# Attention scores in 64-row tiles of the array, two heads per step, with shifted key and score steps

## The chip, the cores and the metric

The kernel runs on one core of a Trainium2 chip. A core has five engines, each with its own queue of instructions, worked off in order: TensorE (PE in the profile, with PEld for the loading of its stationary operand), VectorE (DVE), ScalarE (ACT), GpSimd (POOL) and SyncE (SP, used here only to issue transfers). PE writes to PSUM, and ACT or DVE carry the results from there to SBUF. The metric is the device time of one execution in microseconds.

## The reference

A pooled attention is followed by a maxout feed-forward layer. Eight batches, eight heads, 576 queries of dimension 64. Keys and values are averaged over groups of 8 positions, so that there are 72 of each.

```python
k_p = k.reshape(B, H, Sp, pool, D).mean(axis=3)          # 72 pooled keys
v_p = v.reshape(B, H, Sp, pool, D).mean(axis=3)
scores = scale * np.matmul(q, k_p.transpose(0, 1, 3, 2))  # 576 x 72 per head
attn = np.exp(scores - max); attn = attn / attn.sum(...)
x = np.matmul(attn, v_p)            # heads side by side: 4608 tokens x 512
h = np.maximum(np.maximum(x @ w1, x @ w2), x @ w3)        # 4608 x 768
out = h @ w_out                                           # 4608 x 512
```

## The kernel before, in words

The 4608 tokens are worked in nine blocks of 512 (`block`, line 436). A block has two parts: `hidden` (line 315) forms the three products with w1, w2, w3 for six groups of 128 hidden columns, and `project` (line 327) multiplies by w_out for four groups of 128 tokens. Each part is a generator that yields after each group of matmuls. One such stretch is called a slot here: in `hidden` a slot is four matmuls into a PSUM tile `pw` (line 299), and the slots go round w1, w2, w3; in `project` it is six matmuls into `po` (line 335). Blocks 2 to 8 have 18 + 4 = 22 slots, block 1 has 25 and block 0 has 34, since their first tokens are worked in smaller parts. The tile of w1 is copied to SBUF by ACT (`t`, line 305), VectorE takes the maximum with the second (line 308) and the third (line 311, into `hT`). The tag `pw` has three PSUM buffers.

The attention of a later batch is done between the slots. A plan, a dictionary from slot number to steps, is written out by hand: for block 0 in the call of `block` at line 451, for the others in `plan` (line 460), where block n works on batch n + 1. After a slot's matmuls have been issued, its steps are issued by `do` (line 258), so the place of a step in the plan is its place in the queue of every engine that it uses. The steps that matter here are these.

- `a` (line 281): VectorE adds the two halves of the raw keys of batch 1 into `k16`. `K` (`pool_k`, line 189): four matmuls finish the pooling of these keys in PSUM (`pkp`), and VectorE and then ACT copy them into the two copies in `kps` (lines 196 and 197).
- `k` (`turn_k`, line 183): for batches 1 and 2, six transposes on PE (`pkt`, line 174); for later ones the transposed keys `kT` have been made by a DMA transpose (`Z`, line 272, on SP's queue). Two copies then fill `kz` (line 179), on ACT, for batch 2 on VectorE. `kz` holds for each head the 64 rows of its keys either in partitions 0 to 63 or in 64 to 127 (the parity); the other half is zero. There are two `kz`, for even and odd batches.
- `q` and `Q`: transposes of queries on PE for batch 1, copied out by ACT or VectorE. `T` (line 268): the queries of a later batch by DMA transpose on SP's queue. The transposed queries hold two 64-row groups in the 128 partitions, and a group of 64 queries lies in the lower or upper half by its parity.
- `s` (`scores`, line 213): one head. Three matmuls with all 128 rows (line 203), of 320, 192 and 64 columns; the zero half of `kz` cancels the queries of the other parity. The first has one parity and the other two the other. They fill 576 columns of a PSUM tile `psc` (two banks; tag `att`, two buffers), and ACT takes the exponential of all 576 in one instruction (line 208) into `et`.
- `v` (`values`, line 235): eight matmuls of 65 columns into a tile of tag `att`, reciprocal and multiplication on VectorE into `xn`. `x` and `X` (`turn_x`, line 220): the transpose of `xn` into `xT`, which the next blocks read; on PE for batches 0 and 1, by DMA transpose on SP's queue for the others.

GpSimd loads and pools keys and values of a batch to come (`pool_work`, line 472); its loads wait for the first matmuls of a block. The results go out by DMAs from SP's queue (line 345), the last ones partly from ACT's. For batch 0, before block 0, the scores are formed by functions of their own (lines 381 and 387), which use `score` (line 199).

Of the kernel before, what the change touches and what calls it, by code (L numbers as in the profile page):

```python
# [14 lines left out]
def kernel(  # L15
# [11 lines left out]
    nc = tc.nc  # L27
    dt = mybir.dt
    F32, BF16, F16 = dt.float32, dt.bfloat16, dt.float16

    B, H, S, D = q.shape
    POOL = 8
    Sp = S // POOL
    C = H * D
# [7 lines left out]
    NG = 9  # L42
# [4 lines left out]
    TOK = B * S  # L47
# [7 lines left out]
    psp = ctx.enter_context(tc.tile_pool(name="psp", bufs=1, space=PSUM))  # L55
    ctx.enter_context(tc.manual_schedule())

    kts, vts, qbs, kps, qTs, kTs, ets = {}, {}, {}, {}, {}, {}, {}
# [52 lines left out]
    for i in range(3):  # L111
        if i == 2:
# [5 lines left out]
        out=wo_sb, in_=moe_w_out.rearrange("(jc p) c -> p jc c", p=128))  # L118
# [5 lines left out]
    kz_all = [const.tile([128, 2, H, 128], BF16, name=f"kz{i}", tag=f"kz{i}")  # L124
              for i in range(2)]
# [15 lines left out]
    def new_kp(b):  # L141
        kps[b] = sb2.tile([96, 6, 2, D], BF16, name="kp", tag="kp")
# [17 lines left out]
    def turn_q(b, n0, n1, evac, tag):  # L160
        if b not in qTs:
            qTs[b] = sb2.tile([128, 2 * NG, 128], BF16, name="qT", tag="qT")
        pqt = psp.tile([128, n1 - n0, 128], BF16, name="pqt", tag=tag[0],
                       bufs=tag[1])
        qf = qbs[b].rearrange("p hp t d -> p (hp t d)")
        for n in range(n0, n1):
            nc.tensor.transpose(pqt[:, n - n0, :], qf[:, 128 * n:128 * n + 128],  # L167
                                ident)
        evac(out=qTs[b][:, n0:n1, :], in_=pqt)
# [13 lines left out]
    def turn_k(b):  # L183
        pkt = keys(b, TR) if b < 3 else kTs[b]
        for par in range(2):
            fill_kz(b, par, 0, H, pkt,
                    nc.vector.tensor_copy if b == 2 else nc.scalar.copy)

    def pool_k(b, tag):

        new_kp(b)
        pkp = psp.tile([128, 6, D], F32, name="pkp", tag=tag[0], bufs=tag[1])
        for j in range(4):
            nc.tensor.matmul(pkp, identh[0:96, :], k16[:, :, j, :],  # L194
                             start=(j == 0), stop=(j == 3))
        nc.vector.tensor_copy(out=kps[b][:, :, 0, :], in_=pkp[0:96])
        nc.scalar.copy(out=kps[b][:, :, 1, :], in_=pkp[0:96])

    def score(b, h, out, tp, i0, i1):

        f = NG * (h // 2) + tp
        n = f // 2
        nc.tensor.matmul(out, kz_all[b % 2][:, f % 2, h, :],  # L203
                         qTs[b][:, n + i0:n + i1, 64 * (h % 2):64 * (h % 2) + 64],
                         start=True, stop=True)

    def exp(out, in_):
        nc.scalar.activation(out=out, in_=in_, func=FT.Exp, scale=1.0 / 64.0)  # L208

    def new_et(b):  # L210
        ets[b] = sb2.tile([Sp, H, S], F16, name="et", tag="et")

    def scores(b, h):
        psc = psp.tile([128, 1024], F32, name="psc", tag="att", bufs=2)
        score(b, h, psc[:, 0:320], 0, 0, 5)
        score(b, h, psc[:, 320:512], 1, 0, 3)
        score(b, h, psc[:, 512:576], 1, 3, 4)
        exp(ets[b][:, h, :], psc[0:Sp, 0:S])

    def turn_x(b, c0, keep, xn, tag, evac=nc.scalar.copy):  # L220
        if b > 1:
# [13 lines left out]
    def values(b, c0):  # L235
        pav = psp.tile([128, 2, 512], F32, name="pav", tag="att", bufs=2)
        for h in range(H):
            nc.tensor.matmul(  # L238
                pav[:, h // 4, 65 * (h % 4):65 * (h % 4) + 65],
                ets[b][:, h, c0:c0 + 128], vp_all[:, b, h, :],  # L240
                start=True, stop=True)
        pv = pav[:, :, 0:260].rearrange("p g (h e) -> p g h e", e=65)
        rcp = sb3.tile([128, 2, 4], F32, name="rcp", tag="rcp")
        nc.vector.reciprocal(out=rcp, in_=pv[:, :, :, 64])  # L244
        xn = sb3.tile([128, 2, 4, D], F16, name="xn", tag="xn", bufs=6)
        nc.vector.tensor_tensor(  # L246
            out=xn, in0=pv[:, :, :, 0:D],
            in1=rcp.to_broadcast([128, 2, 4, D]), op=ALU.mult)
        return xn
# [8 lines left out]
    def do(b, steps):  # L258

        for name in steps.split():
            i = int(name[1:] or 0)
            if name[0] in "qQ":
                turn_q(b, *QS[i], nc.vector.tensor_copy if name[0] == "Q"
                       else nc.scalar.copy, TR)
            elif name[0] == "T":
                qTs[b] = sb2.tile([128, 2 * NG, 128], BF16, name="qT", tag="qT")
                nc.sync.dma_start_transpose(  # L270
                    out=qTs[b], in_=qbs[b].rearrange("p hp t d -> p (hp t d)"))
            elif name[0] == "Z":
                kTs[b] = sb2.tile([128, 6, 96], BF16, name="kT", tag="kT")
                nc.sync.dma_start_transpose(
                    out=kTs[b], in_=kps[b].rearrange("p i a d -> p (i a d)"))
            elif name[0] == "k":
                turn_k(b)
            elif name[0] == "K":
                pool_k(b, PW)
            elif name[0] == "a":  # L280
                nc.vector.tensor_tensor(out=k16, in0=kts[b][:, :, 0:4],  # L281
                                        in1=kts[b][:, :, 4:8], op=ALU.add)
            elif name[0] == "s":
                if i == 0:
                    new_et(b)
                scores(b, i)
            elif name[0] == "v":
                xns[b, i] = values(b, CHUNKS[i][0])
            else:
                turn_x(b, *CHUNKS[i], xns[b, i], TR,  # L290
                       nc.vector.tensor_copy if name[0] == "X" else nc.scalar.copy)
# [35 lines left out]
    def project(n, hT):  # L327
        for mm in range(4):
            m = 4 * n + mm
            last = m == TOK // 128 - 1  # L330
            osb = sb3.tile([128, C], F32, name="osb", tag="osb", bufs=5)
            for c in ((slice(0, C // 2), slice(C // 2, C)) if last else (slice(0, C),)):
                po = psp.tile([128, c.stop - c.start], F32, name="po", tag="pw", bufs=3)
                for jc in range(JCH):
                    nc.tensor.matmul(po, hT[:, jc, bass.ts(mm, 128)], wo_sb[:, jc, c],  # L335
                                     start=(jc == 0), stop=(jc == JCH - 1))
                if last:
                    nc.vector.tensor_copy(out=osb[:, c], in_=po)
                else:
                    nc.scalar.copy(out=osb[:, c], in_=po)  # L340
                for u in range(2):
                    b, g = divmod(2 * m + u, NG)
                    dst = out[S * b:S * b + S, :].rearrange("(r g) c -> r g c", g=NG)
                    e = nc.scalar if last and (u or c.start == 0) else nc.sync
                    e.dma_start(out=dst[:, GS[g], c], in_=osb[64 * u:64 * u + 64, c])
            yield

# [15 lines left out]
    for i in range(0, 6, 2):  # L363
        src = kts[0][:, i:i + 2] if i else kt0
        f = const.tile([96, 2, 4, D], F32, name="kf", tag="kf")
# [5 lines left out]
            out=kps[0][:, i:i + 2].rearrange("p i a d -> p a i d"),  # L371
# [64 lines left out]
    def block(n, plan):  # L436
# [3 lines left out]
        for part in (hidden(n, hT), project(n, hT)):  # L440
            for _ in part:
# [7 lines left out]
    fold_v(1)  # L449
    fold_k(2, nc.gpsimd)  # L450
    block(0, {0: [(0, "X1")], 3: [(0, "v2")], 5: [(0, "v3")], 7: [(0, "x2")],
              9: [(0, "x3")], 12: [(0, "v4")], 15: [(0, "x4"), (1, "a")],
              17: [(1, "K")], 19: [(1, "k")], 21: [(1, "q0")],
              22: [(1, "Q1")], 23: [(1, "Q2 s0")], 24: [(1, "Q3 s1")],
              25: [(1, "s2")], 26: [(1, "s3 s4")], 27: [(1, "s5 s6")],
              28: [(1, "s7")], 29: [(1, "v0")], 30: [(1, "v1 x0"), (2, "T")],
              31: [(1, "v2 x1")], 32: [(1, "v3 x2")], 33: [(1, "v4")]})


    def plan(n):  # L460
        b, i = n + 1, 3 * (n == 1)
        got = {0: [], 3: [], (3 + i if n == 1 else 2): [(b, "k")]}
        got.update({5 + i + h: [(b, f"s{h}")] for h in range(H)})
        got[12 + i].append((b + 1, "T"))
        got.update({14 + i + c: [(b, f"v{c} x{c}")] for c in range(5)})
        got[17 + i].append((b + 1, "Z"))
        if n == 1:
            got[0].append((1, "x3"))
            got[3].append((1, "x4"))
        return got  # L470
# [13 lines left out]
    for n in range(1, TOK // NB):  # L484
        block(n, plan(n))
# [30 lines left out]
```

## Time and profile before

| what | us |
|---|---|
| median of six runs (lowest to highest) | 241.34 (240.91 to 243.37) |
| profiled execution: time, and span of its instructions | 240.97, 239.1 |
| granted TensorE clock in the profiled execution | 0.996 of full speed |
| start, until the first transposed queries (to 9.3 us) | 9.3 |
| from there to the end of block 0 (to 49.0) | 39.7 |
| block 1, with batch 2 (49.0 to 73.1) | 24.1 |
| blocks 2 to 6, with batches 3 to 7 | 24.0 to 24.1 each |
| blocks 7 and 8, without attention | 20.7 and 20.8 |
| end, from the last matmul's record on | 4.4 |

The page gives the busy time of each engine in the whole span, the chain of work that ended last, and groups of instructions by line, operation and tile: busy time in us, the mean of one in ns, the idle time of the engine just before them and what ended it. A matmul's record begins when its operand starts to be read and its end is modelled, so the records of consecutive matmuls overlap: the distance from start to start is what a matmul takes of PE's time. The timelines merge neighbouring instructions of the same kind into one line: start, length, engine, line, operation, tiles, how many, and in brackets the idle time before with what ended it.

### The profile page before, as it was taken

What the parts mean: (1) busy time and instruction counts of PE and PEld (TensorE: products, weight loads), DVE (VectorE), ACT (ScalarE), POOL (GpSimd) and SP (SyncE); (2) the same over time, 40 slices, a digit from 0 to 9 for tenths busy, and PEclk for the clock granted to TensorE, in tenths of its full rate; (3) what the DMA queues carried; (4) which work ended last, traced back from release to release, by engine and by line L of the source; (5) the groups of instructions that cost most, each with busy time, mean ns of one, the idle gap of its engine ahead of it and who ended that gap; (6) DMA issues with size and microseconds to landing.
All of it is one profiled execution on the core that took longest, in us unless ns stands there. A gap on an engine that the chain in (4) does not pass through costs nothing.

```text
span 239.1 us, 4202 instructions
## 1 busy us (share of the span) xinstructions
PE 229.7 (96%) x1591; PEld 122.9 (51%) x1591; DVE 123.3 (52%) x231; ACT 112.1 (47%) x184; POOL 123.8 (52%) x91
## 2 busy tenths in 40 slices
PE   7599899999999999999999999999999999999992
PEld 2378755575554555455545554555455544444441
DVE  6767744665672467245724572457245825505531
ACT  2274367546527652765267527652665231142120
POOL 8864275989997479746884688377400000000000
PEclk9999999999999999999999999999999999999998
DMA  7999999999966997699869977997450363034006
GB/s 134 182 196 208 197 201 210 185 164 242 164 139 121 206 205 146 101 222 216 141 108 217 232 159 127 216 204 154 101 132 0 70 137 71 0 83 95 0 21 155
DMA packets 54979, 35.02 MB, mean 146 GB/s; under 512 B 35184, under 2 KB 49520, under 8 KB 54960
## 3 DMA queue, kind: packets, MB, share of 16 engines
q0 software_dynamic: 17088, 17.11, 45.5%
q1 hardware_dynamic: 37632, 17.46, 34.7%
q10 hardware_dynamic: 240, 0.20, 0.4%
q8 instruction: 12, 0.20, 0.3%
q14 instruction: 7, 0.06, 0.1%
HBM read 34.60 MB, written 9.44 MB: 184 GB/s over the span
## 4 chain that ended last, share of the span: by engine, by line
PE 91%; DMA 3%; DVE 2%; ACT 1%; issue 1%; POOL 1%; DVEq 0%; POOLq 0%
PE pw L299 57%; PE po L335 20%; PE psc L203 7%; PE pav L238 4%; DMA qb<-in_q_dram 3%; PE pqt L167 1%; PE pxt L229 1%; PE pvp L156 1%; ACT kz L179 1%; POOL kt L72 1%; PE wm L356 0%; DVE k L281 0%; PE pkp L194 0%; DVE t L308 0%; PE pkt L174 0%
## 5 line engine op out<-in xcount | busy, mean ns | idle before, releaser
L299 PE MATMUL pw<-xT,mw 128*128 128x512 f16 (+2 forms) x708 | 156.1, 361 | 0.2
L299 PEld LDWEIGHTS <-mw 128*128 128x128 f16 x708 | 62.8, 98 | 54.4 <-issue 0.4
L308 DVE TENSOR_TENSOR t<-t,pw 128x512 f16<-128x512 f16 (+2 forms) x59 | 37.9, 642 | 86.5 <-PE pw L299 51.3
L305 ACT CAST t<-pw 128x512 f16<-128x512 f32 (+2 forms) x59 | 32.4, 550 | 44.5 <-PE pw L299 43.0
L335 PE MATMUL po<-mwo,hT 128*128 128x512 f16 (+1 forms) x222 | 49.6, 373 | 0.0
L208 ACT ACTIVATE et<-psc 72x576 f16<-72x576 f32 (+2 forms) x62 | 40.8, 663 | 18.3 <-PE psc L203 18.2
L311 DVE TENSOR_TENSOR hT<-t,pw 128x512 f16<-128x512 f16 (+2 forms) x59 | 37.9, 642 | 9.2 <-PE pw L299 5.2
L340 ACT COPY osb<-po 128x512 f32<-128x512 f32 x35 | 20.5, 586 | 46.0 <-PE po L335 45.3
L135 POOL TENSOR_TENSOR half<-vt 72x2048 f32<-72x2048 f16 x7 | 28.4, 4062 | 10.8 <-DMA vt<-in_v_dram 10.7
L335 PEld LDWEIGHTS <-hT 128*128 128x128 f16 x222 | 20.7, 98 | 22.6 <-DVE hT L311 2.3
L135 POOL TENSOR_TENSOR half<-kt 96x1536 f32<-96x1536 f16 x6 | 18.5, 3086 | 20.3 <-DMA kt<-in_k_dram 20.2
L136 POOL TENSOR_TENSOR half<-half 72x1024 f32<-72x1024 f32 (+1 forms) x13 | 27.2, 2096 | 1.0
L246 DVE TENSOR_TENSOR xn<-pav,rcp 128x512 f16<-128x512 f32 x39 | 27.0, 692 | 1.3
L203 PE MATMUL psc<-qT,kz 128*128 128x64 bf16 (+3 forms) x192 | 25.9, 246 | 0.3 <-DVE kz L179 0.3
L203 PEld LDWEIGHTS <-kz 128*128 128x128 bf16 x192 | 18.0, 98 | 15.6 <-DVE kz L179 0.6
L238 PEld LDWEIGHTS <-et 72*128 72x128 f16 x312 | 15.2, 98 | 7.6
L238 PE MATMUL pav<-vp,et 72*128 72x65 f16 x312 | 16.5, 194 | 0.0
L179 ACT COPY kz<-kT 64x576 bf16<-64x576 bf16 x10 | 11.7, 1168 | 1.3 <-DMA kT<-kp 1.1
L139 POOL TENSOR_TENSOR kp<-half 96x384 bf16<-96x384 f32 x12 | 11.7, 993 | 0.5
L79 POOL DMA_DIRECT2D vt<-in_v_dram x10 | 8.0, 804 | 3.8 <-PE pw L299 2.8
L244 DVE RECIPROCAL rcp<-pav 128x8 f32<-128x8 f32 x39 | 7.8, 201 | 3.2 <-PE pav L238 3.0
L139 POOL TENSOR_TENSOR vp<-half 72x512 f16<-72x512 f32 x7 | 8.9, 1269 | 0.6
(49 smaller groups left out, 78.7 us busy)
## 6 DMA issues: line engine op xcount, KB each, us to landing
out_dram<-osb SPq DMA_DIRECT2D x70, 128.0 KB, 4.6
kt<-in_k_dram POOLq DMA_DIRECT2D x7, 576.0 KB, 6.8
qb<-in_q_dram POOLq DMA_DIRECT2D x7, 576.0 KB, 11.4
vt<-in_v_dram POOLq DMA_DIRECT2D x7, 576.0 KB, 14.7
mw<-in_moe_w_dram POOLq DMA_DIRECT2D x9, 256.0 KB, 9.8
mwo<-in_moe_w_out_dram POOLq DMA_DIRECT2D x1, 768.0 KB, 17.4
qb<-in_q_dram POOLq DMA_DIRECT2D x2, 288.0 KB, 7.1
xT<-xn SPq DMA_TRANSPOSE x30, 2.4
```

Of the source, the lines that this page charges most:

```text
L135: e.tensor_tensor(out=f, in0=t[:, :, 0:4, :], in1=t[:, :, 4:8, :], op=ALU.add)
L136: e.tensor_tensor(out=f[:, :, 0:2, :], in0=f[:, :, 0:2, :], in1=f[:, :, 2:4, :], op=ALU.add)
L139: e.tensor_tensor(out=o, in0=f[:, :, 0, :], in1=f[:, :, 1, :], op=ALU.add)
L203: nc.tensor.matmul(out, kz_all[b % 2][:, f % 2, h, :], qTs[b][:, n + i0:n + i1, 64 * (h % 2):64 * (h % 2) + 64], start=True, stop=True)
L208: nc.scalar.activation(out=out, in_=in_, func=FT.Exp, scale=1.0 / 64.0)
L238: nc.tensor.matmul(pav[:, h // 4, 65 * (h % 4):65 * (h % 4) + 65], ets[b][:, h, c0:c0 + 128], vp_all[:, b, h, :], start=True, stop=True)
L246: nc.vector.tensor_tensor(out=xn, in0=pv[:, :, :, 0:D], in1=rcp.to_broadcast([128, 2, 4, D]), op=ALU.mult)
L299: mm = nc.tensor.matmul(pw, w_sb[wi][:, kc, bass.ts(jc, 128)], xT[:, kc, col], start=(kc == 0), stop=(kc == KCH - 1))
L305: nc.scalar.copy(out=t, in_=pw)
L308: nc.vector.tensor_tensor(out=t1, in0=t, in1=pw, op=ALU.max)
L311: nc.vector.tensor_tensor(out=hT[:, jc, c0:c1], in0=t, in1=pw, op=ALU.max)
L335: nc.tensor.matmul(po, hT[:, jc, bass.ts(mm, 128)], wo_sb[:, jc, c], start=(jc == 0), stop=(jc == JCH - 1))
```

## The change

In `scores` the three matmuls of a head over 128 rows become two over 64 rows: only the half of `kz` and of the queries that belongs to the parity is read, 320 columns for one parity into the first bank of `psc` and 256 for the other into the second. The exponential of a head is taken in two instructions, one for each bank. For batches 2 to 7 a step works on two heads, so that there are four score steps, two slots apart, instead of eight in successive slots; batch 1 keeps one head per step name, but some slots hold two of them.

In the plan of blocks 1 to 6 the scores begin one slot later (slot 6 instead of 5; in block 1 slot 9 instead of 8), the values one slot later, and `k` moves from slot 2 to slot 3 in blocks 2 to 6 (in block 1 it stays at 6). `T` and `Z` keep their slots; `Z` now follows the value chunk 2 instead of 3. In block 0 the steps of batch 1 from `K` to `s6` move by one slot or none, `a` moves two slots forward. The two copies of `pool_k` become one copy on ACT with a broadcast source. In the last group of tokens the 512 columns are split 128 and 384 instead of 256 and 256, and the last transfers are dealt out otherwise to SP's and ACT's queues.

```diff
@@ pool_k
-        nc.vector.tensor_copy(out=kps[b][:, :, 0, :], in_=pkp[0:96])
-        nc.scalar.copy(out=kps[b][:, :, 1, :], in_=pkp[0:96])
+        nc.scalar.copy(out=kps[b].rearrange("p i a d -> p a i d"),
+                       in_=pkp[0:96, None].to_broadcast([96, 2, 6, D]))
@@ scores
-    def scores(b, h):
-        psc = psp.tile([128, 1024], F32, name="psc", tag="att", bufs=2)
-        score(b, h, psc[:, 0:320], 0, 0, 5)
-        score(b, h, psc[:, 320:512], 1, 0, 3)
-        score(b, h, psc[:, 512:576], 1, 3, 4)
-        exp(ets[b][:, h, :], psc[0:Sp, 0:S])
+    def scores(b, hs):
+
+        for h in hs:
+            psc = psp.tile([128, 2, 512], F32, name="psc", tag="att", bufs=2)
+            for tp, m in ((0, 5), (1, 4)):
+                f = NG * (h // 2) + tp
+                rows = slice(64 * (f % 2), 64 * (f % 2) + 64)
+                nc.tensor.matmul(
+                    psc[:, tp, 0:64 * m], kz_all[b % 2][rows, f % 2, h, :],
+                    qTs[b][rows, f // 2:f // 2 + m, 64 * (h % 2):64 * (h % 2) + 64],
+                    start=True, stop=True)
+            exp(ets[b][:, h, 0:320], psc[0:Sp, 0, 0:320])
+            exp(ets[b][:, h, 320:S], psc[0:Sp, 1, 0:256])
@@ do
-                scores(b, i)
+                scores(b, [i] if b < 2 else [2 * i, 2 * i + 1])
@@ project
-            for c in ((slice(0, C // 2), slice(C // 2, C)) if last else (slice(0, C),)):
+            for c in ((slice(0, C // 4), slice(C // 4, C)) if last else (slice(0, C),)):
...
-                    e = nc.scalar if last and (u or c.start == 0) else nc.sync
+                    e = nc.sync
+                    if m >= TOK // 128 - 2 and u != (last and c.start == 0):
+                        e = nc.scalar
@@ block 0
-              9: [(0, "x3")], 12: [(0, "v4")], 15: [(0, "x4"), (1, "a")],
-              17: [(1, "K")], 19: [(1, "k")], 21: [(1, "q0")],
-              22: [(1, "Q1")], 23: [(1, "Q2 s0")], 24: [(1, "Q3 s1")],
-              25: [(1, "s2")], 26: [(1, "s3 s4")], 27: [(1, "s5 s6")],
-              28: [(1, "s7")], 29: [(1, "v0")], 30: [(1, "v1 x0"), (2, "T")],
+              9: [(0, "x3")], 12: [(0, "v4")], 13: [(1, "a")], 15: [(0, "x4")],
+              18: [(1, "K")], 20: [(1, "k")], 22: [(1, "q0")],
+              23: [(1, "Q1")], 24: [(1, "Q2 s0")], 25: [(1, "Q3 s1 s2")],
+              26: [(1, "s3 s4")], 27: [(1, "s5 s6")], 28: [(1, "s7")], 29: [(1, "v0")], 30: [(1, "v1 x0"), (2, "T")],
@@ plan
-        got = {0: [], 3: [], (3 + i if n == 1 else 2): [(b, "k")]}
-        got.update({5 + i + h: [(b, f"s{h}")] for h in range(H)})
+        got = {0: [], 3: [], 3 + i: [(b, "k")]}
+        got.update({6 + i + 2 * h: [(b, f"s{h}")] for h in range(H // 2)})
+        got[13 + i] = []
         got[12 + i].append((b + 1, "T"))
-        got.update({14 + i + c: [(b, f"v{c} x{c}")] for c in range(5)})
+        got.update({15 + i + c: [(b, f"v{c} x{c}")] for c in range(5)})
```

## The prediction

> **What bounds the kernel now.** I read the page first: busy shares (part 1), then the chain that ended last (part 4).
>
> ```profile
> PE 229.7 (96%) x1591; PEld 122.9 (51%) x1591; DVE 123.3 (52%) x231; ACT 112.1 (47%) x184; POOL 123.8 (52%) x91
> PE 91%; DMA 3%; DVE 2%; ACT 1%; issue 1%; POOL 1%; DVEq 0%; POOLq 0%
> ```
>
> TensorE (PE) is the bound and everything else sits near half. What PE saves is saved in the total, and each new gap on PE is paid in full. The groups with shapes kept apart give durations.
>
> ```profile
> L203 PE MATMUL psc<-qT,kz 128*128 128x320 bf16 x56 | 16.7, 299 | 0.0
> L203 PE MATMUL psc<-qT,kz 128*128 128x192 bf16 x56 | 13.8, 246 | 0.0
> L203 PE MATMUL psc<-qT,kz 128*128 128x64 bf16 x64 | 12.1, 193 | 0.0
> L208 ACT ACTIVATE et<-psc 72x576 f16<-72x576 f32 x56 | 36.0, 647 | 16.8 <-PE psc L203 16.8
> L208 ACT ACTIVATE et<-psc 72x1024 f16<-72x1024 f32 x2 | 2.0, 1020 | 1.0 <-PE psc L203 1.0
> L179 ACT COPY kz<-kT 64x576 bf16<-64x576 bf16 x10 | 11.7, 1168 | 1.3 <-DMA kT<-kp 1.1
> ```
>
> The matmul rows differ by 106 ns for 256 columns: 0.415 ns per column, and 166 ns that every record holds whatever its width. Records overlap, so a price on the path must come from starts. The timeline of PE in block 4 (from 121.0 us) gives them.
>
> ```profile
> 120.99 5.34 PE L299 MATMUL pw<-xT,mw 128*128 128x512 f16 x24
> 126.17 0.41 PE L203 MATMUL psc<-qT,kz 128*128 128x320 bf16 x3
> 126.42 1.03 PE L299 MATMUL pw<-xT,mw 128*128 128x512 f16 x4
> 127.28 0.41 PE L203 MATMUL psc<-qT,kz 128*128 128x320 bf16 x3
> ```
>
> One head's scores take 0.25 us (126.17 to 126.42), one slot of four 512-column matmuls 0.86 us, with no gap. Last, the timeline of ScalarE (ACT) in the same block:
>
> ```profile
> 122.06 0.59 ACT L305 CAST t<-pw 128x512 f16<-128x512 f32 x1 [0.28 <-PE pw L299]
> 123.21 2.35 ACT L179 COPY kz<-kT 64x576 bf16<-64x576 bf16 x2 [0.57 <-DMA kT<-kp]
> 125.59 0.59 ACT L305 CAST t<-pw 128x512 f16<-128x512 f32 x1
> 126.62 0.65 ACT L208 ACTIVATE et<-psc 72x576 f16<-72x576 f32 x1 [0.45 <-PE psc L203]
> ```
>
> The two key fills end at 125.56, 0.6 us before the first scores at 126.17. That margin matters below.
>
> The sum is made against the profiled execution: 240.97 us, span 239.1, so 1.9 us around the span; the median of the six runs is 241.34.
>
> **1. Columns.** Batches 1 to 7 have 56 heads of 0.25 us. Each now has a 320- and a 256-column matmul on different halves of the rows, writing different PSUM banks. If the halves stream together, a pair of heads costs 2 x 320 columns x 0.415 ns = 0.27 us instead of 0.50. Batches 2 to 7: 24 pairs x 0.23 = 5.5 us. Batch 1 has five score groups (s0; s1 s2; s3 s4; s5 s6; s7): 0.13 + 3 x 0.27 + 0.13 = 1.1 instead of 2.0, 0.9 saved. Together **-6.4 us**.
>
> **2. Switches between array shapes.** The 29 groups stand between 128-row matmuls, so PE changes shape 58 times. The trace has no such change. Below, nothing: 72-row value matmuls follow 128-row ones without a gap, and a load begun 0.03 us before its matmul (weight load at 126.39, matmul at 126.42) suffices. Above, the earlier matmul must leave the array before the next load starts: 166 + 30 ns, or 166 + 98 (a whole load record) = 0.264 us. I take half of 0.166, 0.083 us: the 166 ns hold a matmul's lead-in and lead-out, and a flush must wait for the lead-out alone; this is the nearest row for a flush, the split is my assumption. In five groups the first switch lies under the wait of step 3, so 53 x 0.083 = **+4.4 us** (ends 0 and +14.0).
>
> The Trainium skill, TensorEngine Tiling (Array Packing), section Tiling Modes, speaks against the change: changing the tiling mode, not just the tile, drains the TensorE. It gives no price, and no run here shows it; were the drain the record's whole 166 ns, step 2 would be 8.8 us. The skill's TensorE: Matmul & The Clock Gate, section Packing small matmuls, says that a weight load overlaps running matmuls only when the row group differs. This trace differs (the load at 125.96 starts under a 128-row matmul, and the next starts on time at 126.17); by that rule the second head's load would wait its 98 ns, 24 x 0.1 = 2.4 us more.
>
> **3. The later key step.** In blocks 2 to 6 (batches 3 to 7) `k` goes from slot 2 to 3, first scores from 5 to 6. Slot 3 also issues a `t` copy, which now stands ahead of the fills on ACT. In block 4's times: slot 3's matmuls end at 121.0 + 4 x 0.86 = 124.46; `t` starts 0.2 later (as at 127.28 to 127.48); fills follow 0.61 after its start and take 2.35: done at 127.62. PE reaches the scores at 121.0 + 7 x 0.86 = 127.05. The first matmul needs only the first fill; the second waits until 127.62, so the group ends at 127.83, not 127.32: 0.51 x 5 = **+2.5 us**. `Z`, the kT transpose, now goes ahead of x3 and x4 on SP's queue (1.2 to 1.6 us each), so kT comes earlier, but fills no longer wait for it. Behind them on ACT, `t` of slot 6 starts 0.4 late; its reader on VectorE needs it 1 us later. Batch 2's fills are on VectorE, and its scores go from 8 to 9: cover grows.
>
> **4. Exps.** The three exp rows (647, 700, 1020 ns for 576, 640, 1024) give 0.83 ns per element and 0.17 fixed: 0.435 and 0.38 for 320 and 256. Four per pair take at most 1.63 us against 1.29; with two thirds of a `t` copy (0.49 apart in the trace), 1.96. PE's two slots and a pair take 1.73 + 0.27 + 0.17 = 2.17: hidden, **0**. If switches were free, PE would take 2.00, so ACT is then just covered too. Without that cover, 0.2 x 24 = 5 us.
>
> **5. Values one slot later.** x0 on SP's queue waited for qT's transpose anyway (133.08 to 138.31, x0 at 138.40; xn was there at 137.66). It comes about 1 us later; the next block needs x2 first in blocks 1 and 2, where x2's transfer is issued near 93.3 and lands 2.4 later, before 97.0. **0**; without cover, up to 1 us in one block. `T` keeps its slot; POOL's loads and folds hang on each block's first matmul, and do not move within it.
>
> **6. Batch 1's front.** In block 0 PE's starts leave three gaps: 0.51 before pkp (27.05; the matmuls before it are out at 26.54), 0.45 before pkt (29.01, against 28.56), 0.23 before pqt (30.81, against 30.58). `a` now runs five slots before `K` instead of two: first gap gone. One ACT copy of 768 elements (0.475 + 384 x 0.83 ns = 0.8) replaces 0.55 on VectorE then 0.47 on ACT: about 0.2 of the second gap stays. q0 comes two slots of 0.86 after `k`, more than the fills' 1.5: third gone. Gain 1.0. Against it, pairs in successive slots (25 to 27) give PE 1.3 us each and ACT 1.2 to 1.6, so 0 to 1 us of waiting for a psc buffer; I take 0.2, since two exps in a row take 1.18 us and not twice 0.647. **-0.8 us**.
>
> **7. The end.** Now ACT's queue issues three transfers of 0.55 us each, the last at 235.8 us. Afterwards each queue has its last ready when the 384-column copy ends: po out at 234.49 + 0.2 + 0.56 (0.29 and 0.425 for 128 and 256) = 235.25. Their 96 KB instead of 64 may take 0.1 longer: **-0.4 us** (0 to -0.5).
>
> Sum: -6.4 + 4.4 + 2.5 - 0.8 - 0.4 = -0.7; 240.97 - 0.7 = **240.3 us**.
>
> **Rivals.** About 1%, 2.4 us, is what a measurement of this kernel can tell from no change.
> - *No change to speak of* (240.3): switches of 0.05 to 0.14 us give -2.5 to +2.3, so 238.5 to 243.3. For it: half of the record's fixed part. 0.38.
> - *Switches nearly free* (0 to 0.03): -5.1 to -3.5, 235.9 to 237.5; the same side if the fills' wait of step 3 does not come (240.3 - 2.5 = 237.8). For it: no gap in the trace at any change of row count; against: none of these changes the array's shape. 0.35.
> - *A full drain* (the other side): at 0.166 to 0.196 per switch, +3.7 to +5.3, 244.7 to 246.3; slower than before from 5.1 / 53 = 0.096 us on. For it: 0.2 us pass between a matmul's last column and the engine that waits for it. 0.17.
> - *The halves do not stream together*, so the change does not do what it says: a pair costs 0.48, a head 0.24, step 1 shrinks to -0.6: +5.1, 246.1. For it: the trace has matmuls following one another only; against: different rows and banks. 0.10.
>
> Faster 0.35, same 0.38, slower 0.27. The range leaves one in ten outside on either side: 236.2 to 246.2. The likeliest case's own range is 238.5 to 243.3.
>
> **What would show it.** Starts of L203's successors: 320- and 256-column matmuls starting a few ns apart, a pair and both switches taking 0.44 us. Per switch: start of the first score matmul against the end of the columns before it, likewise on the way out. A PE wait of about 0.5 us for kz at slot 6 of blocks 2 to 6, named as ACT L179. No gaps before pkp and pqt. Blocks 3 to 6 near 24.0 - 0.9 + 0.6 + 0.5 = 24.2 us each. I am wrong if the switch is far from 0.083 us, if the halves queue, or if the kz wait does not appear.

## The result, and the profile after

The changed kernel takes 242.68 us (median of 29 runs, 241.81 to 246.37) against 241.65 for the kernel before (66 runs). The ratio is 1.0049, with a 95% interval of 1.0029 to 1.0068: 1.2 us slower (0.7 to 1.6). The forecast was 0.7 us faster. The time lies inside the stated range, but it moved the other way.

The profiled execution of the changed kernel took 243.38 us with a span of 241.6. The starts of PE's matmuls at the borders of the blocks, read from the two PE timelines, divide the difference of 2.5 us in the span:

| stretch | before, us | after, us | difference | foretold |
|---|---|---|---|---|
| to the first matmul of block 0 | 17.38 | 18.29 | +0.91 | 0 |
| block 0, with batch 1's front and scores | 30.83 | 30.33 | -0.50 | -0.9 |
| block 1, with batch 2 | 24.75 | 24.69 | -0.06 | -0.3 |
| blocks 2 to 6, with batches 3 to 7 | 120.07 | 122.31 | +2.24 | +0.8 |
| blocks 7 and 8, up to block 8's first `po` matmul | 36.26 | 36.26 | 0.00 | 0 |
| from block 8's first `po` matmul to the end of the span | 9.81 | 9.72 | -0.09 | -0.4 |

The first line is not the change's. The same instructions stand there in both kernels, and PE waits for the first queries from HBM, until 9.29 us before and 10.20 after; in the other profiled executions of this study they came between 8.30 and 10.67. Without it the traces differ by 1.6 us, and the runs by 1.2.

The page of the changed kernel, parts 1 and 4 (the chain by engine and by line):

```profile
PE 231.1 (96%) x1535; PEld 112.7 (47%) x1535; DVE 124.1 (51%) x230; ACT 113.1 (47%) x240; POOL 123.8 (51%) x91
...
PE 86%; ACT 6%; DMA 3%; issue 2%; DVE 1%; POOL 0%; DVEq 0%; POOLq 0%
PE pw L306 53%; PE po L342 19%; ACT kz L179 5%; PE psc L220 4%; PE pav L245 4%; DMA qb<-in_q_dram 3%; PE pxt L236 1%; PE pqt L167 1%; PE psc L203 1%; PE pvp L156 1%; ACT et L208 1%; POOL kt L72 0%; PE wm L365 0%; PE pkt L174 0%; PE pkp L194 0%
```

PE's busy share is 96% as before and tells nothing: a record goes on for 166 ns after its columns have entered and covers a short gap. The chain tells more. ACT holds 6% of it instead of 1%, nearly all of it the key fills, and "issue" has risen to 2%. PE's timeline in block 4 (its first matmul at 122.19) shows both:

```profile
122.19 6.21 PE L306 MATMUL pw<-xT,mw 128*128 128x512 f16 x28
128.33 0.31 PE L220 MATMUL psc<-qT,kz 64*128 64x320 bf16 x1
128.86 0.39 PE L220 MATMUL psc<-qT,kz 64*128 64x256 bf16 x3 [0.23 <-ACT kz L179]
129.19 1.90 PE L306 MATMUL pw<-xT,mw 128*128 128x512 f16 x8
131.02 0.44 PE L220 MATMUL psc<-qT,kz 64*128 64x320 bf16 x4
131.39 1.90 PE L306 MATMUL pw<-xT,mw 128*128 128x512 f16 x8
```

A pair of heads: the columns before it end at 129.19 + 8 x 0.216 = 130.92, its first matmul starts at 131.02, its 0.27 us of columns end at 131.29, and the next matmul starts at 131.39. That is 0.10 + 0.27 + 0.10 = 0.47 us, where two heads took 0.50. The first pair waits for the second fill, from 128.33 to 128.86, and takes 129.19 - 128.24 = 0.95. The cause on ACT, same block:

```profile
125.84 0.59 ACT L312 CAST t<-pw 128x512 f16<-128x512 f32 x1 [2.00 <-PE pw L306]
126.45 2.36 ACT L179 COPY kz<-kT 64x576 bf16<-64x576 bf16 x2
128.83 0.59 ACT L312 CAST t<-pw 128x512 f16<-128x512 f32 x1
```

The fills start 0.61 after the `t` copy that now stands ahead of them and end at 128.81; PE goes on at 128.86. The timeline of the weight loads shows what a switch of shape is:

```profile
130.28 0.31 PEld L306 LDWEIGHTS <-mw 128*128 128x128 f16 x2
131.01 0.11 PEld L220 LDWEIGHTS <-kz 64*128 64x128 bf16 x4 [0.42 <-issue]
131.39 0.11 PEld L306 LDWEIGHTS <-mw 128*128 128x128 f16 x2 [0.26 <-issue]
```

Before the change a load ran ahead of its matmul (scores' loads at 125.96, matmul at 126.17). Now the group's loads begin at 131.01, 0.09 us after the last column of the other shape, and the matmul follows within 0.01. In the list of waits these are two lines, one for each way:

```profile
PEld L220 <- issue: 11.3, 27, 0.4
PEld L306 <- issue: 7.4, 29, 0.4
```

There are 29 score groups; 26 of the first line's waits stand ahead of one and 25 of the second line's behind one. The page blames no instruction ("issue"), since nothing that has a semaphore is being waited for. The lengths in these lines are the loader's idle times, not the cost on the path.

### The profile page after: what moved, and what is told of

Read it like the earlier page. It is cut to its first block, busy times and chain, and to the rows that moved or that the text cites. A ratio compares the mean times of both kernels' runs of the same rounds, so it can differ in the third digit from the quotient of the medians.

```text
span 241.6 us, 4156 instructions
## 1 busy us (share of the span) xinstructions
PE 231.1 (96%) x1535; PEld 112.7 (47%) x1535; DVE 124.1 (51%) x230; ACT 113.1 (47%) x240; POOL 123.8 (51%) x91
## 4 chain that ended last, share of the span: by engine, by line
PE 86%; ACT 6%; DMA 3%; issue 2%; DVE 1%; POOL 0%; DVEq 0%; POOLq 0%
PE pw L306 53%; PE po L342 19%; ACT kz L179 5%; PE psc L220 4%; PE pav L245 4%; DMA qb<-in_q_dram 3%; PE pxt L236 1%; PE pqt L167 1%; PE psc L203 1%; PE pvp L156 1%; ACT et L208 1%; POOL kt L72 0%; PE wm L365 0%; PE pkt L174 0%; PE pkp L194 0%
## 5 line engine op out<-in xcount | busy, mean ns | idle before, releaser
L306 PE MATMUL pw<-xT,mw 128*128 128x512 f16 (+2 forms) x708 | 151.4, 361 | 0.3
L306 PEld LDWEIGHTS <-mw 128*128 128x128 f16 x708 | 64.5, 98 | 68.9 <-issue 7.4
L342 PE MATMUL po<-mwo,hT 128*128 128x512 f16 (+2 forms) x222 | 50.6, 373 | 0.0
L208 ACT ACTIVATE et<-psc 72x320 f16<-72x320 f32 (+2 forms) x118 | 41.1, 427 | 9.4 <-PE psc L220 7.8
L342 PEld LDWEIGHTS <-hT 128*128 128x128 f16 x222 | 20.0, 97 | 21.3 <-DVE hT L318 2.3
L220 PE MATMUL psc<-qT,kz 64*128 64x320 bf16 (+1 forms) x112 | 13.9, 288 | 1.2 <-ACT kz L179 1.2
L220 PEld LDWEIGHTS <-kz 64*128 64x128 bf16 x112 | 3.9, 94 | 14.2 <-issue 11.3
```

Source lines behind the costliest of these rows:

```text
L220: nc.tensor.matmul(psc[:, tp, 0:64 * m], kz_all[b % 2][rows, f % 2, h, :], qTs[b][rows, f // 2:f // 2 + m, 64 * (h % 2):64 * (h % 2) + 64] ...
L306: mm = nc.tensor.matmul(pw, w_sb[wi][:, kc, bass.ts(jc, 128)], xT[:, kc, col], start=(kc == 0), stop=(kc == KCH - 1))
```

## The experiments

All times are ratios to the kernel before, run on the same chip; differences from the changed kernel are differences of ratios (1.0049).

**The key step back in slot 2 (a_k2).**

```diff
-        got = {0: [], 3: [], 3 + i: [(b, "k")]}
+        got = {0: [], 3: [], (3 + i if n == 1 else 2): [(b, "k")]}
```

> The changed kernel with k back in slot 2 in blocks 2 to 6; scores, values and all else as changed. Theory (the loss is the key wait: in each of these blocks PE waits about 0.5 us for the second fill of kz, since a t copy now stands ahead of the fills on ScalarE): the wait goes in five blocks, 0.48 us each between the score group's 0.95 and 0.47 us, so 2.4 us less than the changed kernel, about 0.5% below the kernel before. First rival (the fills only move the wait: ahead of t they hold it back by 1 us, and PE then waits for a pw buffer): the time stays within 0.5 us of the changed kernel. Second rival (the loss is in the switches of array shape alone): no difference either, and the first group's extra time stays.

Measured: 0.9961 (0.9927 to 0.9995), 2.1 us less than the changed kernel. Blocks 2 to 6 take 23.95 us each instead of 24.46. PE's timeline in block 4 (start 122.44) has a first group like the others:

```profile
122.44 6.21 PE L306 MATMUL pw<-xT,mw 128*128 128x512 f16 x28
128.58 0.44 PE L220 MATMUL psc<-qT,kz 64*128 64x320 bf16 x4
128.96 1.90 PE L306 MATMUL pw<-xT,mw 128*128 128x512 f16 x8
```

The theory holds and both rivals fall: the wait is worth 2.1 us by the runs and 2.5 us by the traces, and without it the change is faster than before by about 1 us. The `t` copy behind the fills is late (ready at 126.1, started at 126.49) without a wait on PE.

**The plan's places without the tiles (b_k3).** The kernel before with

```diff
-        got = {0: [], 3: [], (3 + i if n == 1 else 2): [(b, "k")]}
-        got.update({5 + i + h: [(b, f"s{h}")] for h in range(H)})
+        got = {0: [], 3: [], 3 + i: [(b, "k")]}
+        got.update({6 + i + h: [(b, f"s{h}")] for h in range(H)})
...
-        got.update({14 + i + c: [(b, f"v{c} x{c}")] for c in range(5)})
+        got.update({15 + i + c: [(b, f"v{c} x{c}")] for c in range(5)})
```

> The kernel before with the changed plan's places alone: k in slot 3 in blocks 2 to 6, the eight score steps in slots 6 to 13, values one slot later; full-height matmuls, one head per step. Theory (the key wait belongs to the plan and not to the tiles): PE waits for the second kz fill before the second matmul of the first head, 0.5 us in each of five blocks, 2.4 us slower than the kernel before, ratio 1.010. Rival (the wait needs the 64-row groups, since a 128-row matmul waits for nothing new): ratio 1.000.

Measured: 1.0061 (1.0029 to 1.0093), 1.5 us slower. In the trace the wait comes as foretold, with full-height matmuls:

```profile
127.67 0.30 PE L203 MATMUL psc<-qT,kz 128*128 128x320 bf16 x1
128.29 0.28 PE L203 MATMUL psc<-qT,kz 128*128 128x192 bf16 x2 [0.33 <-ACT kz L179]
```

Blocks 2 to 6 grow from 24.01 to 24.54 us, 2.6 us in all; the rival (no wait) falls. The runs show less than the trace, 1.5 us (0.7 to 2.2). The fastest runs of the two differ by 2.5 us (243.11 against 240.65), as the trace does; but the median of the kernel before lies 1.3 us above its fastest run, that of b_k3 only 0.1. What delays the other runs of the kernel before is left open.

**Full-height scores in the better plan (a_k2_full).** `scores` of the kernel before, in the plan of a_k2 with two heads per step.

```diff
-            psc = psp.tile([128, 2, 512], F32, name="psc", tag="att", bufs=2)
...
-            exp(ets[b][:, h, 320:S], psc[0:Sp, 1, 0:256])
+            psc = psp.tile([128, 1024], F32, name="psc", tag="att", bufs=2)
+            score(b, h, psc[:, 0:320], 0, 0, 5)
+            score(b, h, psc[:, 320:512], 1, 0, 3)
+            score(b, h, psc[:, 512:576], 1, 3, 4)
+            exp(ets[b][:, h, :], psc[0:Sp, 0:S])
```

> As a_k2, but every head again by three matmuls with all 128 rows and one exp of 576, two heads per step: only the array's shape and the split of the exp differ from a_k2. Theory (a pair of heads in 64-row tiles takes 0.27 us of columns and twice 0.10 us of switch, against 0.50): 24 pairs x 0.03 us slower than a_k2, less 0.1 in batch 1 where two single heads cost 0.33 against 0.25, so 0.6 us slower than a_k2. Rival (switches dearer than the columns saved): faster than a_k2 by 1 us or more. Rival (switches nearly free, the profile's starts mislead): slower than a_k2 by 4 us or more.

Measured: 0.9977 (0.994 to 1.0013), 0.4 us slower than a_k2, which the runs cannot separate. The traces can: blocks 2 to 6 take 24.01 us against 23.95, block 0 takes 30.09 against 30.33. So the tiles by themselves, the change's main part, gain 0.06 us per block, and lose 0.24 in block 0, where single heads pay two switches each and pairs in successive slots wait for a psc buffer. With block 1 (0.05) that is a net 0.1 us for the tiles, not the 0.6 expected. Both rivals, 1 us faster and 4 us slower, fall.

**Twice as many groups (a_single).** The changed kernel, one head per step in slots 6 to 13.

```diff
-                scores(b, [i] if b < 2 else [2 * i, 2 * i + 1])
+                scores(b, [i])
...
-        got.update({6 + i + 2 * h: [(b, f"s{h}")] for h in range(H // 2)})
+        got.update({6 + i + h: [(b, f"s{h}")] for h in range(H)})
```

> The changed kernel with one head per step in batches 2 to 7, in the eight slots 6 to 13, k still in slot 3: twice as many groups of 64-row tiles, the same matmuls and exps. Theory (each change of shape costs 0.10 us of PE, whatever lies between): 24 more groups, 48 more changes, 4.8 us slower than the changed kernel. Rival (the cost belongs to the group's first loads and shrinks when the loads are fewer): 0.05 each, 2.4 us. Rival (the 0.20 per group is a wait for a psc buffer, not a change of shape): no slower than the changed kernel, since a buffer is free for longer.

Measured: 1.0268 (1.0219 to 1.0318), 5.3 us slower than the changed kernel: 0.11 us for each of 48 switches. The traces give (25.30 - 24.46) / 8 = 0.105.

**A switch by itself (b_tiny64, b_tiny128).** The kernel before with 20 added matmuls of 64 columns whose result is not used, over 64 rows and, as the control, over 128.

```diff
+                if b > 2 and i % 2 == 0:
+                    tiny = psp.tile([128, 64], F32, name="tiny", tag="tr", bufs=1)
+                    nc.tensor.matmul(tiny, warm[0:64, 0:128], warm[0:64, 0:64],
+                                     start=True, stop=True)
                 scores(b, i)
```

> The kernel before with one extra matmul (a constant operand, result not used) of 64 columns over 64 rows ahead of the scores of every second head of batches 3 to 7: 20 extra matmuls, each alone between full-height ones. Theory (each change of shape costs 0.10 us, also without a pair of halves and without kz): 0.03 + 0.20 us each, 4.6 us slower than the kernel before, ratio 1.019; each takes 0.23 us from the end of the columns before to the next start. Rival (the cost belongs to the score groups, to their loads or psc buffers): 0.6 us, ratio 1.003.

> As b_tiny64, with the extra matmul over all 128 rows (the control: same count, same columns, no change of shape). Theory: 20 x 0.03 = 0.6 us slower than the kernel before, ratio 1.002, and no gap on either side. Rival (any extra load and matmul of a new operand leaves a gap): 2 us or more.

Measured: 1.0175 (1.0129 to 1.022) with 64 rows, 1.0014 (0.998 to 1.0048) with 128. The difference is 3.9 us or 0.097 us per switch, with an uncertainty of about a third. In the traces blocks 3 to 6, with eight switches each, take 24.97 and 24.13 us: 0.84 / 8 = 0.105. PE's timelines of the two, first 64 rows:

```profile
125.78 3.19 PE L303 MATMUL pw<-xT,mw 128*128 128x512 f16 x14
128.89 0.20 PE L288 MATMUL tiny<-warm 64*128 64x64 bf16 x1
129.02 0.42 PE L203 MATMUL psc<-qT,kz 128*128 128x320 bf16 x3
```

and 128 rows:

```profile
125.74 1.46 PE L303 MATMUL pw<-xT,mw 128*128 128x512 f16 x6
127.03 0.19 PE L288 MATMUL tiny<-warm 128*128 128x64 bf16 x1
127.06 0.41 PE L203 MATMUL psc<-qT,kz 128*128 128x320 bf16 x3
```

Above, the columns end at 125.78 + 14 x 0.216 = 128.80, then 0.09 pass, 0.03 are the matmul, and 0.10 pass again. Below there is no gap on either side. The price belongs to the switch: not to kz, to psc, or to a pair of halves.

**The four matmuls in another order (a_order).** a_k2 with both heads' 320 columns (one half of the rows) ahead of both heads' 256 columns (the other half).

```diff
-        for h in hs:
-            psc = psp.tile([128, 2, 512], F32, name="psc", tag="att", bufs=2)
-            for tp, m in ((0, 5), (1, 4)):
+        pscs = [psp.tile([128, 2, 512], F32, name="psc", tag="att", bufs=2) for h in hs]
+        for tp, m in ((0, 5), (1, 4)):
+            for h, psc in zip(hs, pscs):
```

> As a_k2, but a pair's four matmuls in another order: both heads' 320 columns (same half of the rows) first, then both heads' 256 columns in the other half. Theory (a matmul streams beside its predecessor only if that is in the other half, and matmuls start in order): the group lasts 0.133 + 0.133 + 0.107 = 0.37 us instead of 0.27, so 27 pairs x 0.1 = 2.7 us slower than a_k2. Rival (PE looks past a matmul that waits for its half): no difference from a_k2. Rival (the halves do not overlap at all, and the short group has another reason): no difference either, with starts one after another in both.

Measured: 0.9954 (0.9922 to 0.9986), as a_k2: my theory's part on the order falls. PE's timeline, in three narrow windows of one group, shows which of the two rivals it is:

```profile
128.10 0.31 PE L220 MATMUL psc<-qT,kz 64*128 64x320 bf16 x2
...
128.22 0.32 PE L220 MATMUL psc<-qT,kz 64*128 64x256 bf16 x2
...
128.24 0.30 PE L220 MATMUL psc<-qT,kz 64*128 64x320 bf16 x1
```

Two matmuls start at 128.10. After they have ended, a 256-column one (from 128.22) and a 320-column one (from 128.24) are left, so the first two were one of each width. In the program the order is 320, 320, 256, 256: the third started with the first, and the fourth ahead of the second. The halves do stream side by side, and a matmul passes one that waits for the other half. The changed kernel shows it too: of its second head in the pair at 131.02, the 256 columns start at 131.14 and the 320 columns at 131.16, though the program has the 320 first. So each half goes through its own matmuls. The pairs of block 0 (`s1 s2`, `s3 s4`, `s5 s6`) have heads of opposite parity, so that each half gets 320 and 256 columns; `s5 s6` takes 0.35 us from its first start to the next full-height matmul (39.01 to 39.36), a pair of like parity 0.37 (131.02 to 131.39).

**Three heads per group (a_three), and two variants.** From a_k2: in batches 2 to 7 groups of 3, 3 and 2 heads, three slots apart. The PSUM buffers are dealt out by width, and one exp takes the same parts of two heads:

```diff
+        g, s = {0: (0, 2), 1: (4, 3), 2: (6, None)}[hs[0]]
+        for u in range(2):
+            tile64(b, g + u, pa[:, u, 0:320], 0)
+            tile64(b, g + u, pb[:, 0, 256 * u:256 * u + 256], 1)
+        if s is not None:
+            pc = psp.tile([128, 256], F32, name="psc1", tag="tr", bufs=1)
+            tile64(b, s, pb[:, 1, 0:320], 0)
+            tile64(b, s, pc, 1)
...
+        got.update({6 + i + 3 * h: [(b, f"s{h}")] for h in range(3)})
```

> As a_k2, but batches 2 to 7 in three groups of 3, 3 and 2 heads, three slots apart, instead of four pairs: the 256-column parts of a pair share a PSUM bank and one exp, the two 320-column parts another exp, a third head's second part lies in the bank of the transposes. Theory (a group costs 0.20 us for its two changes of shape, and the columns of a head 0.133): six groups fewer, 1.2 us faster than a_k2, near ratio 0.991; a group of three takes 0.40 + 0.20 = 0.60. Rival (the psc tiles are no longer doubled, so PE waits for the exps of the group before): as a_k2 or slower, with a PE wait for ACT L208 ahead of the second and third group.

Measured: 0.9937 (0.9907 to 0.9967), with a median of 240.02 us, the fastest of the study by the ratio and faster than both kernels. A group of three takes 0.58 us in PE's timeline, and blocks 2 and 3 take 23.7 us against 23.95 in a_k2. Block 4 of its profiled execution is 1.7 us longer. The list of waits puts this down to ACT's `osb` copy, but that had ended at 143.79, 0.9 us before PE went on at 144.71; the transpose `x1` on SP's queue landed at 144.62 (see step 5 below). The rival's wait for exps does not appear. Against a_k2 the ratio is 0.6 us better; the intervals overlap, but the trace's 0.25 per block has the size of one group less.

`a_three_a` moves one step of block 0:

```diff
-              13: [(1, "a")], 15: [(0, "x4")],
+              15: [(0, "x4"), (1, "a")],
```

> As a_three with the step a of batch 1 back in slot 15 (K stays in slot 18). Theory (in slot 13 the 0.95 us addition on VectorE stands ahead of an hT maximum, and PE waits 0.31 us for a pw buffer before pkp): that gap closes or shrinks, up to 0.3 us faster than a_three. Rival (a in slot 15 delays the next maximum by as much, or k16 comes late for K): no difference, or slower by up to 0.5 us.

Measured: 0.9939 (0.9908 to 0.997), no different from a_three; PE still has a gap of 0.4 us before `pkp`, of which the profile puts 0.23 down to VectorE's `t`. The rival, no difference, holds.

`a_best` gives batch 1 the three full-height matmuls and the single exp of the kernel before:

```diff
-                for tp in range(2):
-                    tile64(b, h, psc[:, tp, 0:320 - 64 * tp], tp)
...
+                score(b, h, psc[:, 0:320], 0, 0, 5)
+                score(b, h, psc[:, 320:512], 1, 0, 3)
+                score(b, h, psc[:, 512:576], 1, 3, 4)
+                exp(ets[b][:, h, :], psc[0:Sp, 0:S])
```

> As a_three, but batch 1 with full-height scores, one head at a time. Theory (a single head in 64-row tiles costs 0.33 us against 0.25, and the split exps keep a pair of batch 1 waiting 0.24 us for a psc buffer): 0.2 to 0.3 us faster than a_three, near ratio 0.992, and block 0 near 30.1 us instead of 30.33. Rival: no difference from a_three.

Measured: 0.9943 (0.9906 to 0.9981), also no different; a gain of 0.25 us is below what the runs separate. Block 0 takes 31.02 us in its trace, of which 1.0 is a wait of PE for the transfer of a weight (`mw`); without it block 0 would be near the expected 30.1. The trace of a_three_a has such a wait of 0.8 in block 0. Neither edit touches that transfer.

**The front and the end alone (b_front_tail).** The kernel before with the changed plan of block 0, the single ACT copy in `pool_k`, and the changed end.

```diff
-              9: [(0, "x3")], 12: [(0, "v4")], 15: [(0, "x4"), (1, "a")],
-              17: [(1, "K")], 19: [(1, "k")], 21: [(1, "q0")],
+              9: [(0, "x3")], 12: [(0, "v4")], 13: [(1, "a")], 15: [(0, "x4")],
+              18: [(1, "K")], 20: [(1, "k")], 22: [(1, "q0")],
...
-            for c in ((slice(0, C // 2), slice(C // 2, C)) if last else (slice(0, C),)):
+            for c in ((slice(0, C // 4), slice(C // 4, C)) if last else (slice(0, C),)):
```

> The kernel before with the changed front of batch 1 in block 0 (a, K, k, q and s slots, one ScalarE copy in pool_k) and the changed end (128 and 384 columns, the other dealing of the last transfers); full-height scores, one head per step, plan of blocks 1 to 6 as before. Theory (the changed kernel's block 0 is 0.5 us shorter and holds 0.1 us of net cost of 64-row groups and 0.24 of a psc wait; its end is 0.1 to 0.4 shorter): 0.8 us faster than before, ratio 0.997. Rival (what the front gives it takes back by a's new place before hT on VectorE, and the end gives nothing): ratio 1.000.

Measured: 0.9977 (0.9946 to 1.0007): 0.6 us faster, with an interval that just reaches no change. In the trace block 0 takes 30.19 us instead of 30.83, and the end 9.73 instead of 9.81. The same trace has blocks 1 and 6 longer by 1.2 and 1.1 us, where scores wait for a late `qT` and key fills for a late `kT`, both DMA transposes that the edit does not touch.

## Why the prediction failed, point by point

The sum was -6.4 + 4.4 + 2.5 - 0.8 - 0.4 = -0.7. Most of its mechanisms were found in the trace; the sign hung on small terms, and the step that failed first is the price of a switch, put at 0.083 us and measured at 0.10; the smaller misses below make up the rest.

- **Columns (step 1): right.** The halves stream together; four matmuls of 1152 columns take 0.27 us. The rival "the halves do not stream together" is out.
- **Switches (step 2): right in kind, too small; with the measured price the sum changes sign.** I took half of the record's fixed 166 ns, 0.083 us, as an assumption. Four readings give 0.09 to 0.11: starts around a group, 0.10; added groups, 0.105 and 0.11; lone matmuls against their control, 0.097 by the runs and 0.105 by the traces. With 0.10, 53 switches cost 5.3 us instead of 4.4, and the sum is +0.2. The forecast had named 0.096 as the point from which the change loses, so a step whose size was an assumption stood 0.013 from it. That the whole record's 166 ns must be waited for (the full-drain rival) is refuted as well. The Trainium skill, TensorEngine Tiling (Array Packing), section Tiling Modes, says that a change of mode drains the TensorE. These runs agree and give the price it leaves out. The rule from TensorE: Matmul & The Clock Gate, section Packing small matmuls, that a load overlaps only with matmuls in another row group, does not hold here: the group's four loads start within 0.02 us (131.01 to 131.03), the last two while a matmul runs in each half. The same section says that matmuls start in program order without exception, and a_order and the changed kernel show one passing another.
- **The key step (step 3): right in place and size.** Foretold: the wait ends 6.62 us after the block's start, 0.51 each. Measured: PE goes on 6.67 after it, the group takes 0.48 more than the others, and undoing the move gives 2.1 us back (2.5 by the traces).
- **Exps (step 4): right.** 434 and 380 ns, four in 1.30 us; PE waits for none of them in blocks 1 to 6.
- **Values later (step 5): put at 0, and 0.1 us in this trace; the cover is thin.** In block 4 the transpose `x1`, issued behind the 4.8 us of `qT`'s on SP's queue, lands at 146.65, and block 5 starts at 146.74, 0.11 us after PE was free for it. Four of the eight other profiled executions with the values in the later slots (a_order, a_three, a_three_a, a_best) lose 0.4 to 1.7 us there, each time starting block 5 0.09 us after `x1` landed; the four with the old slots lose nothing there. How often this happens without the profiler is not known.
- **The front (step 6): too large.** The gaps before pkt and pqt went as foretold (0.18 left, none left), and pkp follows without one. But a new gap of 0.30 us stands one slot ahead of it (27.45 to 27.75). VectorE's addition (26.42 to 27.37) now stands ahead of an `hT` maximum (27.29 in place of about 26.6, by my estimate), and PE waits for a pw buffer. I had moved an instruction past others on VectorE's queue without asking who waits for those. Moving it back (a_three_a) left a gap of 0.4 before pkp.
- **The end (step 7): too large**, 0.1 instead of 0.4. The 384-column copy ended as foretold, 5.95 us after block 8's first `po` matmul. But ACT's queue was still issuing the transfer before (0.73 us) and issued its last one 0.24 after the copy, and that took 2.30 us to land instead of 2.10; I had counted 0 and 0.1 for these.

By the traces, the size of the switch accounts for about 0.9 us of the 2.3 between -0.7 and +1.6, the end for 0.3, the front without its switches for 0.2. The rest, about 0.9 us, lies mostly in blocks 2 to 6: the waiting group is 0.07 us longer than step 3 with the right switch would have it (0.95 against 0.88), and a head took 0.2475 us before and not 0.25. Of the 0.45 us that each of these blocks gained, the groups' starts explain 0.38. The first full-height matmul behind each group takes 0.226 us to the next start instead of 0.216, which makes 0.04 per block, and block 4 holds the 0.11 of step 5.

So the change combined a gain of 0.5 to 0.6 us from batch 1's front, a gain from the tiles that the switches nearly eat up (0.06 us per block of four pairs), and a loss of 2.1 to 2.5 us from moving `k` by one slot, which the tiles do not need.

## What to carry to other kernels

Before packing small matmuls into parts of the array, count the changes of shape in the order of issue and set 0.1 us against each; the columns saved between two changes must be worth more than 0.2 us, so gather as much as the PSUM banks allow into each group (three heads here instead of two). When a step moves in a plan, write down what then stands ahead of it on its own engine: one copy ahead of the fills cost several times what the tiles brought. A sum that rests on an assumed size should be given with its break-even beside it, and no sign claimed when the two are that near.

## What the runs showed of the hardware

- A change between matmuls over 128 rows and over 64 rows leaves PE without columns for 0.09 to 0.10 us each way, and no load is pulled ahead across it: the loads start at 131.01, the columns before end at 130.92. Changes between 128 and 72 or 96 rows showed no gap.
- Matmuls in the two halves of the rows run side by side, and one can pass an earlier one that waits for the other half (a_order). So TensorE does not work off its queue strictly in order, though the section on the chip says so of every engine.
- PE's busy share stayed at 96% although about 5 us of gaps were added, because the modelled ends of the records cover them. Starts, and the loader's "issue" waits, show them.
